# Spreading an ELU chain over two iterations of a fused attention and two-layer expert kernel

## The chip, the cores and the metric

The kernel runs on one core of one Trainium2 chip. The metric is the device time of one launch in microseconds, lower is better; a kernel's time is the median of its runs.

## What is computed

Three stages follow each other, all in float32. The first is attention in chunks of 32 queries, with 8 memory keys and a window of 16 keys to the left and 8 to the right, for 4 batches, 8 heads, 768 tokens and a head size of 64. Its output, 3072 tokens by 512, goes through a feed-forward layer with an ELU, and that through a second layer without one:

```python
h = x @ w_in                                   # 512 -> 2048
g = np.where(h > 0.0, h, np.exp(np.minimum(h, 0.0)) - 1.0)
x = g @ w_out                                  # 2048 -> 512
a = x @ w1
b = x @ w2
out = ((a * b) @ w3) @ w_out2                  # 512 -> 1024 -> 1024 -> 512
```

## The kernel before

**Numbers.** Every float32 operand of a large matmul is split in a high part and a low part, and each product is three matmuls (`mm3`, L129 to L131). The weights arrive as 64-bit numbers: a job of the `feed` (`rebase` L164, `shift` L168, `low` L172, `hi_of` L177, `lo_of` L180) turns the two words of each into float32 and then into the high and low part. ScalarE (ACT) does `rebase` and `hi_of`, VectorE (DVE) the other three. Jobs for the weights of the first layer run while the loop below runs its first iterations. Jobs for the weights of the second layer (`mid_jobs`) are spread between the attention groups, and their results are stored back to DRAM.

**The main loop.** It has 130 iterations n. Each handles one block of 128 of the 2048 inner columns for 384 tokens. `mm_h(n)` makes a block h in one of two PSUM banks (12 matmuls of 384 columns; bank n % 2), `elu_exp(n)` takes it through relu (L484) and exp (L485) on ACT, `elu_split(n)` forms the ELU with a maximum on DVE (L491, called max below; it is the last reader of the bank), its high part on ACT (hi, L125) and its low part on DVE (lo, L126), and `mm_x(n)`, which is issued two iterations later, multiplies the result by w_out. So `mm_h(n + 2)` waits for max(n), and `mm_x(n)` for lo(n).

**What runs between.** Each iteration takes two slots of the attention, one behind `mm_h` and one behind `mm_x` (`at_step`). A group G of 128 queries takes about ten slots: transposes of q and k (`at_turn`, `at_turn2`, copied out by ACT in L298 to L311), scores (L322 on TensorE), maximum, subtraction and exponential (`at_max`: L339 and L340 on DVE, L341 on ACT), sums and normalization (L347 to L359), a transpose on DVE (`at_flip`, L370), the product with v (L381), and the copy into the next block of x (`at_out`). The slots of each group are set by `paces` and `base`; every engine runs its own instructions in the order in which this Python code issues them, and SyncE (SP) issues nearly all DMAs, also in that order.

**Blocks.** After 8 or 16 iterations the 384 tokens of the block are done. In the first two iterations of the next block, called F and F + 1 here, `mm_x` and its slot come ahead of `mm_h` (`first`). In iteration F + 1 the four output banks are copied out (`store_x1`: L120 twice on ACT, L122 twice on DVE) into tiles of the pool `f_p`, which has four buffers and is shared with the weight jobs, and each copy is stored by a DMA (L506). From the sixth block on, the blocks have 16 iterations, and five of them, from iterations 32, 48, 64, 80 and 96, begin with an attention group.

Of the kernel before, what the change touches and what calls it, by code (L numbers as in the profile page):

```python
# [8 lines left out]
F32 = mybir.dt.float32  # L9
F32R = mybir.dt.float32r  # L10
I32 = mybir.dt.int32
AF = mybir.ActivationFunctionType
ALU = mybir.AluOpType
# [6 lines left out]
def tile_kernel(  # L20
# [23 lines left out]
    nc = tc.nc  # L44
    P = 128
# [13 lines left out]
    TB = 384  # L59
    NB = NT // TB  # L60
    GPB = TB // GQ
    FF1 = w_in.shape[1] // P
# [19 lines left out]
    g_p = ctx.enter_context(tc.tile_pool(name="g_p", bufs=3))  # L82
# [41 lines left out]
    def split(hi, lo, src):  # L124
        nc.scalar.copy(hi, src)  # L125
        nc.vector.tensor_tensor(out=lo, in0=src, in1=hi.bitcast(F32), op=ALU.subtract)  # L126
# [314 lines left out]
    others = [Job((raw_rows, w_out2, c, 0), store=wod[c]) for c in range(FF2)]  # L441
# [3 lines left out]
    for G in range(GPB, NG):  # L445
        s0, pace = base(G)
        for at, fn in zip(paces[pace], chain):
            put(s0 + at, fn, G)
        if G >= GM:
            n = [(G - GM + i) * n_others // (NG - GM) for i in range(2)]  # L450
            for job, at in zip([others.pop(0) for _ in range(n[1] - n[0])], (0, 5)):
                mid_jobs.append(job)
                for i, fn in enumerate((rebase, mid_low, mid_split)):
                    put(s0 + at + i, fn, job)
                if at == 0 and w3s and pace == "slow":
                    job = w3s.pop(0)
                    mid_jobs.append(job)
                    for at3, fn in ((3, rebase), (4, mid_low), (9, mid_flip)):
                        put(s0 + at3, fn, job)
    assert not others and not w3s  # L460
    slot_at = [0]
# [1 line left out]
    def at_step():  # L463
        store_next()
        for _, _, fn, arg in sorted(slots.pop(slot_at[0], ()), key=lambda x: x[:2]):
            fn(arg)
        slot_at[0] += 1


    h_t, eg_t, g_t = {}, {}, {}  # L470
# [3 lines left out]
    def mm_h(n):  # L474
        j, f = seq[n][:2]
        ph, w, x = PS[4 + n % 2][:, 0:TB], W[f], xhl[j % 2]
        for i in range(KT):
            c = slice(i * P, (i + 1) * P)
            mm3(ph, w[:, 0, c], w[:, 1, c], x[:, 0, i, :], x[:, 1, i, :], i == 0, i == KT - 1)
        h_t[n] = ph  # L480

    def elu_exp(n):
        e = eg_p.tile([P, TB], F32, tag="eg", name="eg")
        nc.scalar.activation(e, h_t[n], AF.Relu, scale=-1.0)  # L484
        nc.scalar.activation(e, e, AF.Exp, scale=-1.0)  # L485
        eg_t[n] = e

    def elu_split(n):
        ph, e = h_t.pop(n), eg_t.pop(n)
        g = g_p.tile([P, 2, TB], F32R, tag="g", name="g")  # L490
        nc.vector.scalar_tensor_tensor(out=e, in0=e, scalar=-1.0, in1=ph, op0=ALU.add, op1=ALU.max)  # L491
        split(g[:, 0, :], g[:, 1, :], e)
        g_t[n] = g

    def mm_x(n):
        f, at, last = seq[n][1:]
# [83 lines left out]
    with tc.manual_schedule():  # L580
        def weight(i):
            if i < FF1:
                return Job((raw_cols, w_in, i), slot=i)
            return Job((raw_rows, w_out, i - FF1, 0), slot=i)

        jobs, due = [], {}
        order = sorted(range(2 * FF1), key=lambda i: (i % FF1 // HALF, i if i < FF1 else i - FF1 + 2))
        for i in order:
            due[i] = len(jobs)
            jobs.append(weight(i))  # L590
        first_late = min(due[i] for i in LATER)
        feed = Feed(jobs)

        load_qk(0)
        make_identity(nc, ident)
        nc.gpsimd.memset(kn[0:LEFT, 0], 0.0)
        nc.gpsimd.memset(vw[0:LEFT, 0], 0.0)
        for c in range(NCG):
            for s in range(2):
                nc.gpsimd.memset(odd[c * CH:(c + 1) * CH, s], float(c % 2 == s))  # L600
        feed.load(1)
        load_qk(1)
        feed.load(2)
        load_v(0)
        load_qk(2)
        load_v(1)
        feed.load(3)
        load_v(2)
        feed.load(5)
        one = dict(t=at_turn, u=at_turn2, s=at_scores, m=at_max, z=at_sum, n=at_norm, p=at_flip, v=at_values, o=at_out)  # L610
        for what in START.split():
            if what == "f":
                feed.step()
            else:
                one[what[0]](int(what[1]))
        load_qk(GPB)
        load_v(GPB)
        early_psum.close()
        psum_x = ctx.enter_context(tc.tile_pool(name="psum_x", bufs=1, space=PSUM))
        for i in range(KT):  # L620
            PS[i] = psum_x.tile([P, 512], F32, name=f"bank{i}")
        NH = NB * FF1
        for n in range(NH + 2):
            j, f, at, last = seq[n] if n < NH else (NB, n - NH, n - NH, False)
            first = at < 2 and n >= 2
            if j == NB - 1 and f == 0:
                store_next()
                mid_ctx.close()
                at_ctx.close()
                late = ctx.enter_context(tc.tile_pool(name="late", bufs=1, side="right"))  # L630
                ab_jobs = [(c, r) for c in range(FF2) for r in range(2)]
            if n == FF1 + 2:
                feed.until(len(feed.jobs) - 1)
                raw_ctx.close()
                mid_ctx = ExitStack()
                pools["raw"] = mid_ctx.enter_context(tc.tile_pool(name="raw2", bufs=2, side="right"))
                pools["st"] = mid_ctx.enter_context(tc.tile_pool(name="st_p", bufs=2, side="right"))
                mid_load(2)

            def x():  # L640
                if n >= 2:
                    if n < 3 * FF1 // 2 + 2:
                        feed.until(due[FF1 + seq[n - 2][1]])
                    mm_x(n - 2)
                    if at == 1 and n < NH:
                        p = n // HALF - 1
                        store_x1(seq[n - 2][0], x1p if p < 2 else x1d)
                if n < FF1 + 2:
                    feed.step()
                at_step()  # L650

            if first:
                x()
            if n < NH:
                if j == 0:
                    feed.until(due[f])
                mm_h(n)
                elu_exp(n)
                if n < FF1 + 2:
                    feed.step()  # L660
                at_step()
            if not first:
                x()
            if n < NH:
                elu_split(n)
            if n >= NH - FF1:

                free = [f] if n < NH else []
                if n >= NH - FF1 + 2:
                    free.append(FF1 + n - 2 - (NH - FF1))  # L670
                for slot in free:
                    if len(s_wo) < FF2 and len(s_wo) <= len(s_w3):
                        fill(slot, wod[len(s_wo)])
                        s_wo.append(slot)
                    elif len(s_w3) < 2 * FF2:
                        half, c = divmod(len(s_w3), FF2)
                        fill(slot, w3d[half][c])
                        s_w3[half, c] = slot
                    else:
                        c, r = ab_jobs.pop(0)  # L680
                        fill(slot, wabd[c][r])
                        s_ab[c, r] = slot
            if j == NB - 1:
                if f == 4:
                    load_x1(0)
                if f == 8:
                    split_x1(0)
                    load_x1(1)
        store_x1(NB - 1, x1d)
        for half in range(2):  # L690
            for c in range(FF2):
                for i in range(KT):
                    mm_wc(half, c, i)
                    if c == FF2 - 1:
                        keep_wc(half, i)
            for i in range(KT, FF2):
                c, r = ab_jobs.pop(0)
                fill(s_w3[half, i], wabd[c][r])
                s_ab[c, r] = s_w3[half, i]
        NA = NB * FF2  # L700
        for n in range(NA + 1):
            j, f = divmod(n, FF2)
            if n < NA:
                mm_ab(n)
                if f == 2 and j + 1 < NB:
                    split_x1(j + 1)
                    if j + 2 < NB:
                        load_x1(j + 2)
            if n >= 1:
                mm_o(n - 1)  # L710
                if f == 0:
                    store_out(j - 1)
# [30 lines left out]
```

## Time and profile before

| | us |
|---|---|
| median of 3 runs (1163.06 to 1166.07) | 1163.41 |
| profiled execution, its own time | 1165.6 |
| profiled execution, span from first to last instruction | 1163.8 |
| TensorE matmul busy | 1101.9 (95%) |
| TensorE weight load busy | 1038.8 (89%) |
| VectorE busy | 500.8 (43%) |
| ScalarE busy | 432.0 (37%) |

In the rows below, PE is TensorE, PEld its weight load, DVE VectorE, ACT ScalarE and SPq the queue of SyncE. A row of a timeline has the start, the duration, the engine, the line, what it writes and reads, shapes and count, and in brackets how long the engine was idle before it and what ended that. The first 40 us hold the attention of the first three groups; the main loop runs from 39.8 to 713 us, its weight jobs until about 154 us and its attention until about 645 us; the second layer follows. Times of shares are averages over stages with different limits, so the stretches are read apart.

### The profile page before, as it was taken

Reading aid. Unit: us, or ns where it says so; the run is one execution under the profiler, and the core shown is the slowest. Engines: PE = TensorE matmul, PEld = TensorE weight load, DVE = VectorE, ACT = ScalarE, POOL = GpSimd, SP = SyncE. Lnnn points to the kernel's source line nnn. Section 1 sums busy time; section 2 is a strip of 40 time slices with the busy share of each in tenths; the row PEclk is TensorE's granted clock in tenths of the full one; section 3 lists DMA queues with packets and bytes.
Section 4 is the critical chain, followed back from the end, with each engine's and each line's share of the span. In section 5 each row is a group of like instructions: output and inputs, shape, how many; then the busy total and the mean of one; then the engine's idle time right before and its main releaser. Section 6 shows DMA issues by size and latency. Waiting matters only on the chain.

```text
span 1163.8 us, 20920 instructions
## 1 busy us (share of the span) xinstructions
PE 1101.9 (95%) x8800; PEld 1038.8 (89%) x8800; DVE 500.8 (43%) x924; ACT 432.0 (37%) x901; POOL 2.1 (0%) x16
## 2 busy tenths in 40 slices
PE   4667899999999999999999999999999999999998
PEld 3557898989999989989999999799999999999997
DVE  4677745655655655565655341032212212122221
ACT  3444654444545544554454441031212212122111
POOL 0000000000000000000000000000000000000000
PEclk7677999999999999999999999999999999999999
DMA  8934624354454544543542696320100101000000
GB/s 188 253 90 128 205 81 130 118 154 124 141 155 124 153 151 119 158 134 115 167 126 71 232 327 218 109 64 11 44 28 28 55 1 55 28 28 28 1 28 28
DMA packets 155405, 127.94 MB, mean 110 GB/s; under 512 B 104112, under 2 KB 138928, under 8 KB 155312
## 3 DMA queue, kind: packets, MB, share of 16 engines
q1 hardware_dynamic: 154272, 126.35, 36.1%
q8 instruction: 69, 1.13, 0.4%
q10 hardware_dynamic: 1040, 0.26, 0.1%
q14 instruction: 24, 0.20, 0.1%
HBM read 91.46 MB, written 35.13 MB: 109 GB/s over the span
## 4 chain that ended last, share of the span: by engine, by line
PE 84%; DVE 7%; ACT 3%; DMA 2%; issue 2%; SPq 1%; DVEq 0%; ACTq 0%
PE bank L129 22%; PE bank L131 21%; PE bank L130 21%; PE banks L129 4%; PE banks L130 4%; PE banks L131 4%; PE banks L381 2%; PE banks L322 1%; DMA x1d<-st 1%; DVE e L359 1%; DVE w L180 1%; DVE f L172 1%; PE banks L294 1%; PE banks L296 1%; DVE eg L491 1%
## 5 line engine op out<-in xcount | busy, mean ns | idle before, releaser
L129 PE MATMUL bank<-xhl,w 128*128 128x384 f32 x768 | 266.9, 348 | 10.6 <-DVE eg L491 10.0
L131 PE MATMUL bank<-xhl,w 128*128 128x384 f32 x768 | 260.9, 340 | 0.0
L130 PE MATMUL bank<-xhl,w 128*128 128x384 f32 x768 | 260.6, 339 | 0.0
L125 ACT CAST g<-eg 128x384 fp32r<-128x384 f32 x192 | 98.4, 512 | 310.8 <-DVE eg L491 171.7
L129 PE MATMUL bank<-g,w 128*128 128x384 f32 x512 | 178.1, 348 | 0.0
L131 PE MATMUL bank<-g,w 128*128 128x384 f32 x512 | 173.0, 338 | 0.0
L130 PE MATMUL bank<-g,w 128*128 128x384 f32 x512 | 172.9, 338 | 0.0
L126 DVE TENSOR_TENSOR g<-eg,g 128x384 fp32r<-128x384 f32 x192 | 107.2, 558 | 141.9 <-ACT g L125 141.9
L129 PEld LDWEIGHTS bank<-xhl,w 128*128 128x128 f32 x768 | 146.3, 191 | 19.4 <-DVE eg L491 13.6
L561 DVE TENSOR_TENSOR eg<-eg,banks 128x384 f32<-128x384 f32 x64 | 35.5, 555 | 267.2 <-PE banks L131 267.2
L130 PEld LDWEIGHTS bank<-xhl,w 128*128 128x128 f32 x768 | 146.6, 191 | 3.2 <-DVE xhl L126 0.4
L131 PEld LDWEIGHTS bank<-xhl,w 128*128 128x128 f32 x768 | 146.5, 191 | 0.0
L129 PEld LDWEIGHTS bank<-g,w 128*128 128x128 f32 x512 | 97.4, 190 | 2.3
L130 PEld LDWEIGHTS bank<-g,w 128*128 128x128 f32 x512 | 97.6, 191 | 0.0
L131 PEld LDWEIGHTS bank<-g,w 128*128 128x128 f32 x512 | 97.4, 190 | 0.0
L560 ACT COPY eg<-bank 128x384 f32<-128x384 f32 x64 | 30.7, 480 | 168.1 <-PE bank L131 168.1
L484 ACT ACTIVATE eg<-bank 128x384 f32<-128x384 f32 x128 | 62.6, 489 | 67.0 <-PE bank L131 67.0
L491 DVE SCALAR_TENSOR_TENSOR eg<-eg,bank 128x384 f32<-128x384 f32 x128 | 69.7, 545 | 39.0 <-ACT eg L485 38.7
L129 PE MATMUL banks<-xhl,w 128*128 128x384 f32 x256 | 85.5, 334 | 0.0
L130 PE MATMUL banks<-xhl,w 128*128 128x384 f32 x256 | 85.5, 334 | 0.0
L131 PE MATMUL banks<-xhl,w 128*128 128x384 f32 x256 | 85.5, 334 | 0.0
L131 PE MATMUL bank<-w,g 128*128 128x512 f32 x192 | 76.0, 396 | 0.0
(100 smaller groups left out, 1303.6 us busy)
## 6 DMA issues: line engine op xcount, KB each, us to landing
raw<-in_moe_w_dram SPq DMA_DIRECT2D x32, 512.0 KB
raw<-in_moe_w_out_dram SPq DMA_DIRECT2D x19, 512.0 KB
w3d<-st SPq DMA_DIRECT2D x16, 512.0 KB
wabd<-st SPq DMA_DIRECT2D x16, 512.0 KB
w<-w3d SPq DMA_DIRECT2D x16, 512.0 KB
w<-wabd SPq DMA_DIRECT2D x16, 512.0 KB
raw<-in_moe_w_in_dram SPq DMA_DIRECT2D x13, 512.0 KB
x1d<-st SPq DMA_DIRECT2D x32, 192.0 KB
```

What stands on the lines that cost most here:

```text
L125: nc.scalar.copy(hi, src)
L126: nc.vector.tensor_tensor(out=lo, in0=src, in1=hi.bitcast(F32), op=ALU.subtract)
L129: mm(o, lhsT=w_hi, rhs=x_hi, start=start, stop=False)
L130: mm(o, lhsT=w_hi, rhs=x_lo, start=False, stop=False)
L131: mm(o, lhsT=w_lo, rhs=x_hi, start=False, stop=stop)
L172: nc.vector.scalar_tensor_tensor(out=t, in0=l, scalar=29, in1=t, op0=ALU.logical_shift_right, op1=ALU.bitwise_or)
L180: nc.vector.tensor_tensor(out=job.to[:, 1, :], in0=job.f if src is None else src, in1=job.to[:, 0, :].bitcast(F32), op=ALU.subtract)
L381: mm(o, lhsT=vw[cc, u, 2 * hp + r, :], rhs=pT[cc, r, hp, u, :], start=u == 0, stop=u == 1)
L484: nc.scalar.activation(e, h_t[n], AF.Relu, scale=-1.0)
L491: nc.vector.scalar_tensor_tensor(out=e, in0=e, scalar=-1.0, in1=ph, op0=ALU.add, op1=ALU.max)
L560: nc.scalar.copy(e, pab[0])
L561: nc.vector.tensor_tensor(out=e, in0=e, in1=pab[1], op=ALU.mult)
```

## The change

The chain of one block h is no longer issued at the end of one iteration. Relu and exp of block n move behind the attention slot that follows `mm_h(n)`; max stays at the end of the iteration; hi and lo of block n move into iteration n + 1, right behind `mm_h(n + 1)`, with a step of the weight feed between them while there is one. The second mid job of a group starts one slot later (6 for 5), and `rebase` and `low` of its job for w3 one slot later (4 and 5 for 3 and 4). The instructions themselves, their shapes and TensorE's order are the same.

```diff
-            for job, at in zip([others.pop(0) for _ in range(n[1] - n[0])], (0, 5)):
+            for job, at in zip([others.pop(0) for _ in range(n[1] - n[0])], (0, 6)):
...
-                    for at3, fn in ((3, rebase), (4, mid_low), (9, mid_flip)):
+                    for at3, fn in ((4, rebase), (5, mid_low), (9, mid_flip)):
...
-    def elu_split(n):
-        ph, e = h_t.pop(n), eg_t.pop(n)
-        g = g_p.tile([P, 2, TB], F32R, tag="g", name="g")
-        nc.vector.scalar_tensor_tensor(out=e, in0=e, scalar=-1.0, in1=ph, op0=ALU.add, op1=ALU.max)
-        split(g[:, 0, :], g[:, 1, :], e)
-        g_t[n] = g
+    def elu_max(n):
+        e = eg_t[n]
+        nc.vector.scalar_tensor_tensor(out=e, in0=e, scalar=-1.0, in1=h_t.pop(n), op0=ALU.add, op1=ALU.max)
+
+    def elu_hi(n):
+        g_t[n] = g_p.tile([P, 2, TB], F32R, tag="g", name="g")
+        nc.scalar.copy(g_t[n][:, 0, :], eg_t[n])
+
+    def elu_lo(n):
+        g = g_t[n]
+        nc.vector.tensor_tensor(out=g[:, 1, :], in0=eg_t.pop(n), in1=g[:, 0, :].bitcast(F32), op=ALU.subtract)
...
                 mm_h(n)
+            if 1 <= n <= NH:
+                elu_hi(n - 1)
+            if n < FF1 + 2:
+                feed.step()
+            if 1 <= n <= NH:
+                elu_lo(n - 1)
+            at_step()
+            if n < NH:
                 elu_exp(n)
-                if n < FF1 + 2:
-                    feed.step()
-                at_step()
             if not first:
                 x()
             if n < NH:
-                elu_split(n)
+                elu_max(n)
```

In the changed kernel max is L490, hi is L494 and lo is L498. Three places show what moves.

ACT in iteration 1, from the attention's exponential (L341) on; `eg` is the tile of the ELU, `w` a weight's tile, `f` the working tile of a weight job. Before:

```order
L341 ACTIVATE e<-e 128x512
L125 CAST g<-eg 128x384
L484 ACTIVATE eg<-bank_96 128x384
L485 ACTIVATE eg<-eg 128x384
L177 CAST w_85<-f 128x512
L164 ACTIVATE f<-more 128x512
```

and now:

```order
L341 ACTIVATE e<-e 128x512
L494 CAST g<-eg 128x384
L177 CAST w_85<-f 128x512
L164 ACTIVATE f<-more 128x512
L484 ACTIVATE eg<-bank_96 128x384
L485 ACTIVATE eg<-eg 128x384
```

The weight job's two instructions stood behind relu and exp of block 1 and now stand ahead of them.

ACT in iteration 48, the first of a block (F), from the copies of the turned q on. Before, hi of block 47 stood first:

```order
L125 CAST g<-eg 128x384
L298 COPY qT<-banks 128x512
L301 COPY kT<-banks 128x16x32
L302 COPY kT<-banks 128x4x3x24
L164 ACTIVATE f<-raw 128x512
L484 ACTIVATE eg<-bank_95 128x384
```

and now:

```order
L298 COPY qT<-banks 128x512
L301 COPY kT<-banks 128x16x32
L302 COPY kT<-banks 128x4x3x24
L164 ACTIVATE f<-raw 128x512
L494 CAST g<-eg 128x384
L309 COPY kT<-banks 128x4x24
L311 COPY kT<-banks 128x16x8
L484 ACTIVATE eg<-bank_95 128x384
```

Hi of block 47 moved behind three copies of the attention and a `rebase`.

ACT in iteration 49 (F + 1), from the copies of the outputs (`st`) on. Before:

```order
L120 COPY st<-bank_597 128x384
L120 COPY st<-bank_599 128x384
L177 CAST st<-f 128x512
L484 ACTIVATE eg<-bank_96 128x384
L485 ACTIVATE eg<-eg 128x384
L341 ACTIVATE e<-e 128x512
L164 ACTIVATE f<-raw 128x512
L125 CAST g<-eg 128x384
```

and now:

```order
L120 COPY st<-bank_597 128x384
L120 COPY st<-bank_599 128x384
L177 CAST st<-f 128x512
L494 CAST g<-eg 128x384
L341 ACTIVATE e<-e 128x512
L484 ACTIVATE eg<-bank_96 128x384
L485 ACTIVATE eg<-eg 128x384
L494 CAST g<-eg 128x384
L164 ACTIVATE f<-raw 128x512
```

Relu and exp of block 49 moved behind the attention's exponential L341, and hi of block 48 came down from the iteration before.

## Rows read from the trace of the kernel before

**Rows 1.** Busy time by stretch: us, each engine's busy (x), clock, DMA share, GB/s.

```profile
110.47:154.00 43.53, 39.45 (x256) 38.35 (x257) 33.15 (x62) 28.14 (x55) 0.00 (x0) 0.90 0.53 159
245.00:650.00 405.00, 399.12 (x4076) 381.43 (x4076) 230.60 (x430) 197.77 (x421) 0.00 (x0) 1.00 0.45 134
```

**Rows 2.** Waits of PE from 250 to 650: us in total, times, longest.

```profile
PE bank L129 <- DVE eg L491: 5.9, 6, 1.3
```

**Rows 3.** Timeline of ACT in the first two iterations.

```profile
44.46 0.49 ACT L484 ACTIVATE eg<-bank 128x384 f32<-128x384 f32 x1 [4.71 <-PE bank L131]
...
52.30 0.49 ACT L125 CAST g<-eg 128x384 fp32r<-128x384 f32 x1
54.37 0.49 ACT L484 ACTIVATE eg<-bank 128x384 f32<-128x384 f32 x1 [1.57 <-PE bank L131]
...
55.33 0.60 ACT L177 CAST w<-f 128x512 fp32r<-128x512 f32 x1
```

**Rows 4.** Timeline of DVE at the same place.

```profile
55.97 0.69 DVE L180 TENSOR_TENSOR w<-f,w 128x512 fp32r<-128x512 f32 x1 [1.51 <-ACT w L177]
```

**Rows 5.** Timeline of PE, at the products with v of three groups.

```profile
62.10 0.38 PE L381 MATMUL banks<-pT,vw 64*64 64x64 f32 x4 [5.50 <-DVE pT L370]
...
110.47 0.39 PE L381 MATMUL banks<-pT,vw 64*64 64x64 f32 x4 [4.08 <-DVE pT L370]
...
213.38 0.34 PE L381 MATMUL banks<-pT,vw 64*64 64x64 f32 x7 [0.96 <-DVE pT L370]
```

**Rows 6.** Timeline of ACT in iteration 5.

```profile
92.99 0.49 ACT L484 ACTIVATE eg<-bank 128x384 f32<-128x384 f32 x1 [1.24 <-PE bank L131]
...
95.02 0.56 ACT L298 COPY qT<-banks 128x512 f32<-128x512 f32 x1
```

**Rows 7.** Timeline of DVE in iterations 10 and 11.

```profile
136.39 0.55 DVE L491 SCALAR_TENSOR_TENSOR eg<-eg,bank 128x384 f32<-128x384 f32 x1
137.52 0.56 DVE L126 TENSOR_TENSOR g<-eg,g 128x384 fp32r<-128x384 f32 x1 [0.58 <-ACT g L125]
...
141.33 0.55 DVE L491 SCALAR_TENSOR_TENSOR eg<-eg,bank 128x384 f32<-128x384 f32 x1
```

**Rows 8.** Timeline of DVE at the block that begins with iteration 48.

```profile
330.43 0.56 DVE L122 COPY st<-bank 128x384 f32<-128x384 f32 x1 [2.97 <-ACT eg L484]
...
332.45 0.69 DVE L340 TENSOR_TENSOR e<-banks,mx 128x512 f32<-128x512 f32 x1
333.06 0.55 DVE L491 SCALAR_TENSOR_TENSOR eg<-eg,bank 128x384 f32<-128x384 f32 x1
334.80 0.56 DVE L126 TENSOR_TENSOR g<-eg,g 128x384 fp32r<-128x384 f32 x1 [1.20 <-ACT g L125]
...
338.79 0.55 DVE L491 SCALAR_TENSOR_TENSOR eg<-eg,bank 128x384 f32<-128x384 f32 x1
```

**Rows 9.** Timeline of PE at the same block, iteration 52.

```profile
339.39 0.44 PE L129 MATMUL bank<-xhl,w 128*128 128x384 f32 x1 [1.17 <-DVE eg L491]
```

**Rows 10.** Timeline of ACT at the same block.

```profile
319.96 0.51 ACT L125 CAST g<-eg 128x384 fp32r<-128x384 f32 x1 [1.22 <-DVE eg L491]
...
323.36 0.68 ACT L164 ACTIVATE f<-raw 128x512 f32<-128x512 f32 x1
...
329.94 0.49 ACT L484 ACTIVATE eg<-bank 128x384 f32<-128x384 f32 x1 [2.26 <-PE bank L131]
330.46 0.53 ACT L485 ACTIVATE eg<-eg 128x384 f32<-128x384 f32 x1
333.18 0.63 ACT L341 ACTIVATE e<-e 128x512 f32<-128x512 f32 x1 [2.19 <-DVE e L340]
```

**Rows 11.** Issues of SP at the same block.

```profile
325.60 0.37 SPq L145 DMA_DIRECT2D raw<-in_moe_w_dram  x1
326.81 4.53 SPq L506 DMA_DIRECT2D x1d<-st  x4
```

**Rows 12.** Waits of DVE from 245 to 600: us in total, times, longest.

```profile
DVE st L122 <- DMA x1d<-st: 13.5, 4, 4.1
```

**Rows 13.** Timeline of DVE at the block that begins with iteration 96.

```profile
573.55 0.56 DVE L122 COPY st<-bank 128x384 f32<-128x384 f32 x1 [2.00 <-DMA x1d<-st]
```

**Rows 14.** Busy time of PE by stretch, as rows 1.

```profile
132.06:135.20 3.14, 3.14 (x13) 0.67 0.47 160
118.30:128.80 10.50, 10.50 (x62) 1.00 0.68 227
```

## The prediction

> **What bounds the kernel now.** I looked first at busy time by stretch, since the change touches only the main loop. From 245 to 650 us TensorE is busy for 399.1 of 405 us at the full clock, while VectorE and ScalarE are busy for about half [rows 1]. So there the change can win at most the few stalls of TensorE, and the list of its waits holds one cause, 5.9 us in six waits for max to free a bank of h [rows 2]. The rest is to be had before 154 us, where the timelines show TensorE waiting for VectorE and these two for ScalarE. I read the timelines at the two kinds of place where TensorE stalls: the ramp (40 to 154 us), where weight jobs compete with the ELU, and the starts of blocks.
>
> **The ramp: what is removed.** ScalarE's queue runs in order, and relu(n) is the one instruction in it that waits for `mm_h(n)`: 4.71 us in iteration 0, 1.57 in iteration 1 [rows 3]. What stands behind waits too: in iteration 1 the cast L177 of a weight starts at 55.33, and VectorE waits for it until 55.97 [rows 3, 4], with the attention's sums, normalization and transpose behind; TensorE gets the transposed tile only at 62.10 after 5.50 us of idling [rows 5].
>
> Term 1. In the new order L177 follows hi(0) directly. Hi starts at 52.30; the maximum behind which it waits comes some 0.4 us earlier, because relu(0) no longer holds the first copies. So hi starts at 51.9, L177 at 52.3 instead of 55.33, 3.0 us earlier. VectorE now does lo(0) behind that cast, 0.5 us, which leaves 2.5 us at L381: 59.6 for 62.10.
>
> Term 2. From there to the next group's product each lo loses its wait for hi, because a weight step stands between them now; two such waits of about 0.6 us, less some delay of a weight cast behind relu and exp, leave 0.8 us. Sum 3.3.
>
> Term 3. In iteration 5 the copy L298 runs at 95.02 behind relu (92.99, waiting for TensorE), exp and a weight step [rows 6]. It needs only transposes that TensorE runs right behind the block whose end released relu, so by about 93.4, and now it stands ahead of relu: 1.6 us. Another shorter wait of lo gives 0.5. At 110.47 [rows 5] the gain is 5.4 us.
>
> Term 4. From iteration 10 to 15 VectorE sets the pace: from max to max 4.94 us, with only one idle piece of 0.58, lo waiting for hi [rows 7]. With a weight step between them that piece goes, and 4.36 us remain; TensorE's own two blocks of 12 matmuls take 4.1 (62 in 10.5 us at the full clock [rows 14]), so VectorE still sets it. Four iterations give 2.3 us. The ramp gains 5.4 + 2.3 = 7.7 us. As bounds I take 5 (terms 1 and 4 alone) and 9.5 (blocks like that at 132.06, which ran at 0.67 of the clock [rows 14], might be spared it).
>
> **Behind the ramp** no step of the feed stands between hi and lo, so VectorE waits for hi as before, and nothing is won in the middle of a block: TensorE has no wait there. What is moved is relu and exp, behind the attention slot, and max with them.
>
> **The starts of blocks: what is added.** In iteration F + 1 VectorE's second copy of the outputs must wait until the DMA of the first copy has landed; four of the five starts show it as such, 13.5 us in all [rows 12], the fifth under another name: 2.97 us until 330.43 [rows 8]. With it the scores' maximum and L340 wait (332.45) and ScalarE's L341 (333.18) [rows 8, 10]. Before, relu and exp of block F + 1 (329.94, 330.46) ran while VectorE waited [rows 10], so max(F + 1) went right behind L340, at 333.06. Now they stand behind L341. From the copy at 330.43, t0, step by step: L340 at 2.0, plus lo(F), which now also stands behind the copy, 0.5: t0 + 2.5. L341 0.73 later (332.45 to 333.18): 3.2. L341, relu and exp at 0.5 each, and 0.1: max(F + 1) at t0 + 4.85. Lo(F + 1) starts 1.13 behind max, as in [rows 7]: 5.98. From lo to max(F + 2) the work is unchanged, 334.80 to 338.79, 3.99: t0 + 9.97. Before it was 338.79 - 330.43 = 8.36. So max(F + 2) is 1.6 us later, and the matmul that already waits for it, `mm_h(F + 4)` at 339.39 [rows 9], with it; queued behind that are the group's L381 and all that follows.
>
> And t0 itself moves. Hi(F - 1) ran at 319.96 and now stands behind the rebase at 323.36, so at 323.9 [rows 10]; lo(F - 1) behind it starts at about 324.5 and pushes the weight job's work, and with it the load issued at 325.60, by 0.9 us, while the first store, issued at 326.81 [rows 11], moves by 0.1 only. If the landing goes by the store's own issue, t0 moves 0.1; if the load ahead of it in the queue sets it, 0.9. I take 0.6, nearer to the load, since load and store leave 1.2 us apart on one queue and land together only 3.6 us later.
>
> [...]
>
> Per start 1.6 + 0.6 = 2.2 us, five starts 11.0 us. The start at iteration 96 has no TensorE wait in the trace, but max there is done just before its matmul, so it pays nearly all. As bounds for one start: 1.0 (the two L120 no longer stand behind hi(F), so the store could leave and land 0.6 earlier) and 2.7.
>
> One group more, at 213.38 [rows 5]: its L340 stands in the same iteration as an output copy, lo(24) now waits for a hi behind L341 and holds the sums. That adds 0.9 us (bounds 0 and 1).
>
> **Edits at nothing.** The jobs that start one slot later issue the same instructions and loads; before 650 us VectorE is idle for 43% of the time [rows 1], which hides them. Without that cover one slip of L168 and L172 would cost about 1 us in a group. The number of instructions, TensorE's order and the second layer stay.
>
> **Sum.** -7.7 + 11.0 + 0.9 = +4.2 us, on the profiled execution's own 1165.6: 1169.8 us. That execution is 2.2 above the median of 1163.41, so I forecast **1167.6 us**.
>
> **Rivals.**
> 1. The two sides cancel. If a start costs only its lower bound, 1.1 with the change of t0, five give 5.5: -7.7 + 5.5 + 0.9 = -1.3, 1162.1 us. For it: the store's copies do come free of hi(F). Against it: the load's delay, and that relu behind L341 is in the order itself.
> 2. Faster: the starts cost next to nothing, because the store lands early. At iteration 96 the same copy waited 2.00 us [rows 13], against up to 4.1 at the others [rows 12]; if the earlier copies let all stores land so, t0 would fall by about 1.5 us and pay for the longer chain: -7.7 + 0.9 = -6.8, 1156.6 us. It decides from a cost per start under 0.7 us. Against it: load and store stand closer together on the queue, not further apart.
> 3. Slower still: TensorE's clock. After a wait of 3.15 us at 132 us the next 3.14 us ran at 0.67 of the clock and the block took 3.14 instead of 2.03 [rows 14], 1.1 us lost. After the present waits of up to 1.3 us at block starts the clock stays at 1.00 [rows 1, 2]. With several waits of 0.6 to 1.5 us in a row at each start it might fall: 5 x 1.1 = 5.5 us more, 1173.1.
>
> [...] The trace at block starts does not agree so far, hence its low chance.
>
> **How the numbers follow.** Less than 0.3%, 3.5 us, can hardly be told from no change here. Forecast 0.50, its own range 1164 to 1172; rival 1 0.24; rival 2 0.15; rival 3 0.11. Faster takes rival 2 and a little of 1: 0.19. Same takes the rest of 1 and the low edge of the forecast: 0.27. Slower is 0.54. The range of 1157 to 1173.5 leaves out about half of rival 3 and a part of rival 2.
>
> **What the profile would show.** Right: L381 near 59.6 and 105 us; lo without a wait in the ramp; iteration 15's block some 7 to 8 us earlier; then at each of the five starts relu directly behind L341, max(F + 1) about 2 us later against the output copy, and TensorE's waits for max (now L490) grown from 6 to about 15 us or more, some under `mm_x` waiting for lo (L498). Wrong: waits of TensorE at the starts unchanged or gone; a ramp that ends no earlier, with a new wait for relu in it; a clock under 1.00 behind 245 us; or stalls in the middle of blocks, where max now follows the attention's work.

## The result: slower by 0.65%, a ramp that gains and block starts that lose more

| | us |
|---|---|
| before, median of 5 runs beside the changed kernel | 1163.41 (1159.81 to 1166.07) |
| after, median of 5 runs | 1170.6 (1169.24 to 1172.9) |
| ratio, with its 95% interval | 1.0065 [1.0042, 1.0089] |
| after, profiled execution: own time, span | 1170.6, 1168.8 |

First the busy time by stretch of the kernel after, with the columns of [rows 1], and its waits of TensorE from 250 to 650 us, as [rows 2]:

```profile
110.47:154.00 43.53, 40.73 (x219) 40.16 (x218) 31.74 (x59) 26.80 (x53) 0.00 (x0) 0.93 0.47 145
245.00:650.00 405.00, 391.97 (x3960) 371.69 (x3959) 229.16 (x425) 196.32 (x413) 0.00 (x0) 1.00 0.44 131
```

```profile
PE bank L129 <- DVE eg L490: 10.9, 10, 1.4
PE bank L130 <- DVE g L498: 0.9, 2, 0.5
```

From 245 us on TensorE is busy 7 us less than in [rows 1], at the same clock of 1.00. Its waits for max have nearly doubled against [rows 2], from 5.9 to 10.9 us and from six to ten, two at each of the five starts, and waits for lo are new.

**The ramp.** TensorE at the products with v, against [rows 5]:

```profile
61.52 0.37 PE L381 MATMUL banks<-pT,vw 64*64 64x64 f32 x4 [4.44 <-DVE pT L370]
...
106.57 0.38 PE L381 MATMUL banks<-pT,vw 64*64 64x64 f32 x4 [3.51 <-DVE pT L370]
...
124.62 0.44 PE L129 MATMUL bank<-g,w 128*128 128x384 f32 x1 [1.38 <-ACT g L494]
126.47 0.69 PE L130 MATMUL bank<-g,w 128*128 128x384 f32 x1 [1.42 <-DVE g L498]
...
207.81 0.29 PE L381 MATMUL banks<-pT,vw 64*64 64x64 f32 x4 [0.64 <-DVE pT L370]
```

The three products with v come 0.6, 3.9 and 5.6 us earlier than before. In between stand two waits that [rows 5] has no partner for: at 124.62 for hi, at 126.47 for lo. ScalarE in iterations 1 and 5, against [rows 3, 6]:

```profile
53.85 0.50 ACT L494 CAST g<-eg 128x384 fp32r<-128x384 f32 x1
54.26 0.61 ACT L177 CAST w<-f 128x512 fp32r<-128x512 f32 x1
54.78 0.67 ACT L164 ACTIVATE f<-more 128x512 f32<-128x512 f32 x1
55.35 0.47 ACT L484 ACTIVATE eg<-bank 128x384 f32<-128x384 f32 x1
...
90.14 0.58 ACT L298 COPY qT<-banks 128x512 f32<-128x512 f32 x1 [1.40 <-PE banks L296]
...
92.33 0.51 ACT L484 ACTIVATE eg<-bank 128x384 f32<-128x384 f32 x1
```

L177 follows hi, and L298 stands ahead of relu. Relu waits for nothing in either place; in [rows 3, 6] it held the queue for 1.57 and 1.24 us. VectorE at the cast of [rows 4], and at max in iterations 9, 10 and 13 (against [rows 7]):

```profile
54.90 0.69 DVE L180 TENSOR_TENSOR w<-f,w 128x512 fp32r<-128x512 f32 x1 [0.16 <-ACT w L177]
...
126.62 0.55 DVE L490 SCALAR_TENSOR_TENSOR eg<-eg,bank 128x384 f32<-128x384 f32 x1 [0.20 <-ACT eg L485]
...
131.02 0.55 DVE L490 SCALAR_TENSOR_TENSOR eg<-eg,bank 128x384 f32<-128x384 f32 x1
...
144.20 0.55 DVE L490 SCALAR_TENSOR_TENSOR eg<-eg,bank 128x384 f32<-128x384 f32 x1
```

The wait of 1.51 us at L180 has shrunk to 0.16, and from max to max it is now 4.40 us (131.02 - 126.62; four intervals take 17.58).

**A start of a block**, iteration 48, as [rows 8 to 12]. VectorE first, then TensorE, ScalarE, the issues, and VectorE's waits from 245 to 600 us:

```profile
327.43 0.56 DVE L122 COPY st<-bank 128x384 f32<-128x384 f32 x1 [4.16 <-DMA x1d<-st]
...
328.75 0.53 DVE L498 TENSOR_TENSOR g<-eg,g 128x384 fp32r<-128x384 f32 x1
...
329.92 0.69 DVE L340 TENSOR_TENSOR e<-banks,mx 128x512 f32<-128x512 f32 x1
332.30 0.55 DVE L490 SCALAR_TENSOR_TENSOR eg<-eg,bank 128x384 f32<-128x384 f32 x1 [1.69 <-ACT eg L485]
333.44 0.56 DVE L498 TENSOR_TENSOR g<-eg,g 128x384 fp32r<-128x384 f32 x1 [0.58 <-ACT g L494]
...
337.55 0.55 DVE L490 SCALAR_TENSOR_TENSOR eg<-eg,bank 128x384 f32<-128x384 f32 x1
```

```profile
332.91 0.45 PE L129 MATMUL bank<-xhl,w 128*128 128x384 f32 x1 [1.38 <-DVE eg L490]
...
338.15 0.44 PE L129 MATMUL bank<-xhl,w 128*128 128x384 f32 x1 [0.81 <-DVE eg L490]
```

```profile
330.70 0.63 ACT L341 ACTIVATE e<-e 128x512 f32<-128x512 f32 x1 [6.24 <-DVE e L340]
331.24 0.47 ACT L484 ACTIVATE eg<-bank 128x384 f32<-128x384 f32 x1
331.75 0.52 ACT L485 ACTIVATE eg<-eg 128x384 f32<-128x384 f32 x1
```

```profile
322.71 0.37 SPq L145 DMA_DIRECT2D raw<-in_moe_w_dram  x1
323.19 2.06 SPq L511 DMA_DIRECT2D x1d<-st  x2
```

```profile
DVE st L122 <- DMA x1d<-st: 15.7, 4, 4.2
```

Relu and exp, which ran in the shadow of the store's landing in [rows 10], now stand behind L341 while ScalarE idles 6.24 us ahead of it. From the copy at 327.43 max(F + 2) takes 10.12 us, for 8.36 in [rows 8]. That is 1.76 more, and it is 1.76 more at each of the other four starts too, when the same two rows are read there. The store leaves 0.48 us behind the load, for 1.21 in [rows 11].

### The profile page after: what moved, and what is told of

It reads as the page before. It is cut to its first block, busy times and chain, and to the rows that moved or that the text cites. A ratio compares the mean times of both kernels' runs of the same rounds, so it can differ in the third digit from the quotient of the medians.

```text
span 1168.8 us, 20946 instructions
## 1 busy us (share of the span) xinstructions
PE 1104.1 (94%) x8800; PEld 1038.0 (89%) x8800; DVE 500.8 (43%) x924; ACT 434.5 (37%) x901; POOL 2.1 (0%) x16
## 4 chain that ended last, share of the span: by engine, by line
PE 83%; DVE 7%; DMA 4%; ACT 4%; issue 2%; SPq 1%; DVEq 0%; ACTq 0%
PE bank L129 22%; PE bank L130 21%; PE bank L131 21%; PE banks L129 4%; PE banks L130 4%; PE banks L131 4%; PE banks L381 2%; DMA x1d<-st 2%; PE banks L322 1%; DMA kn<-in_k_dram 1%; DVE g L498 1%; DVE e L359 1%; PE banks L296 1%; PE banks L294 1%; PE banks L308 1%
## 5 line engine op out<-in xcount | busy, mean ns | idle before, releaser
L129 PE MATMUL bank<-xhl,w 128*128 128x384 f32 x768 | 265.7, 346 | 11.6 <-DVE eg L490 10.9
L498 DVE TENSOR_TENSOR g<-eg,g 128x384 fp32r<-128x384 f32 x128 | 71.3, 557 | 101.1 <-ACT g L494 101.1
L494 ACT CAST g<-eg 128x384 fp32r<-128x384 f32 x128 | 65.7, 513 | 124.9 <-DVE eg L490 124.9
L490 DVE SCALAR_TENSOR_TENSOR eg<-eg,bank 128x384 f32<-128x384 f32 x128 | 69.8, 545 | 57.7 <-ACT eg L485 57.4
```

The source lines that it names most:

```text
L129: mm(o, lhsT=w_hi, rhs=x_hi, start=start, stop=False)
L494: nc.scalar.copy(g_t[n][:, 0, :], eg_t[n])
L498: nc.vector.tensor_tensor(out=g[:, 1, :], in0=eg_t.pop(n), in1=g[:, 0, :].bitcast(F32), op=ALU.subtract)
```

## The experiments

All twelve were timed in several runs beside the kernel before, on one chip for each set of four (before: 1162.24, 1162.14 and 1161.52 us). All fourteen kernels run the same 8800 matmuls in the same order, so one time can be read at the same matmul in each trace. **A** is the L381 at 213.38 of [rows 5], and its time is what the ramp costs. **B** is a matmul near the end of the main loop (690.72 us before, 695.76 after). Between A and B lie the five starts. From B to its last matmul every execution takes the same 468.9 us.

| kernel | median us | ratio to before | A | A to B |
|---|---|---|---|---|
| before | 1163.4 | 1 | 213.4 | 477.4 |
| after | 1170.6 | 1.0065 [1.0042, 1.0089] | 207.8 | 488.0 |
| e1 new order in the ramp only | 1155.6 | 0.9948 [0.9930, 0.9966] | 205.9 | 474.1 |
| e2 new order behind the ramp only | 1175.5 | 1.0118 [1.0101, 1.0135] | 213.1 | 487.6 |
| e3 exp ahead of the attention step | 1157.7 | 0.9968 [0.9955, 0.9981] | 202.5 | 479.2 |
| e4 hi and lo ahead of the copies | 1168.8 | 1.0058 [1.0037, 1.0079] | 207.0 | 487.1 |
| e5 exp ahead of the feed's step too | 1170.7 | 1.0074 [1.0061, 1.0086] | 218.0 | 478.8 |
| e6 before, packed copies | 1156.1 | 0.9951 [0.9937, 0.9964] | 211.4 | 468.1 |
| e7 after, packed copies | 1152.5 | 0.9917 [0.9904, 0.9931] | 208.5 | 471.0 |
| e8 e1, packed copies | 1148.5 | 0.9885 [0.9871, 0.9899] | 204.8 | 468.1 |
| e9 before, exp behind the feed's step | 1156.2 | 0.9947 [0.9927, 0.9966] | 204.9 | 474.1 |
| e10 before, new job slots | 1162.1 | 1.0001 [0.9988, 1.0014] | 210.7 | 474.3 |
| e11 e9, packed copies | 1150.9 | 0.9905 [0.9884, 0.9926] | 207.6 | 468.1 |
| e12 e3, packed copies | 1149.6 | 0.9893 [0.9874, 0.9912] | 205.6 | 470.5 |

One execution's A is uncertain. Four programs with the order of before up to there have 213.4, 211.4, 210.7 and 213.1 (mean 212.2); five with the new order have 204.8 to 208.5 (mean 206.8). A part of that is TensorE's clock: from the first to the second product of [rows 5] the order of before took 48.4 and 49.1 us in two executions where the granted clock in between was 0.82 and 0.81, and 45.5 and 45.7 us in two where it was 0.88 and 0.87. The execution of before that was costed is one of the first two; why its clock was lower was not looked into. A to B repeats within 0.5 us for an order, with one exception: the profiled execution of before, 477.4, where three others of the same order there have 474.1 to 474.3.

**e1 and e2: the two halves apart.** The new order stands while `n < FF1 + 2` (18, as long as the feed runs) in e1, whose lines against the changed kernel follow, and only from there on in e2, with the two branches exchanged; the job slots are those of the order behind the ramp:

```diff
+            if n < FF1 + 2:
+                if n >= 1:
+                    elu_hi(n - 1)
                 feed.step()
+                if n >= 1:
+                    elu_lo(n - 1)
+                at_step()
...
+            else:
...
+                if n < NH:
+                    elu_exp(n)
+                at_step()
...
                 elu_max(n)
+                if n >= FF1 + 2:
+                    elu_hi(n)
+                    elu_lo(n)
```

> The new order of the ELU's steps (and of the job slots) only as long as the feed runs, iterations 0 to 17; from iteration 18 on the order and the slots of before. Theory: the change is two separate effects, a gain in the ramp and a loss at the five starts of blocks. Then this kernel keeps the gain that the changed kernel showed by 213 us, 5.6 us, and pays nothing behind it: 1163.4 - 5.6 = 1157.8 us, ratio 0.995. Rival A: the earlier end of the ramp is of no use, since loads of the middle part then come too late and TensorE waits for them: about 1163. Rival B: the loss at the starts comes from the ramp (what was moved forward collides there), not from the order behind it: about 1170.

> The order of before in iterations 0 to 17, the new order (and the new job slots) from 18 on. Theory: pays the five starts in full and gains nothing: 1163.4 + 10.4 = 1173.8 us, ratio 1.009; TensorE's stall for the maximum at each start grows from about 1 to about 3 us in two pieces. Rival: if the starts are dear only because the ramp ended earlier, about 1163.

Measured: 1155.6 and 1175.5. TensorE's waits from 245 to 650 us in e2:

```profile
PE bank L129 <- DVE eg L490: 10.8, 10, 1.4
PE bank L130 <- DVE g L498: 2.2, 6, 0.9
```

Both rivals of e1 and that of e2 fall: the gain and the loss are separate, and they add: -0.52% and +1.18% give +0.66%, where the whole change has +0.65%. e2's loss is above what I expected, 13.3 us between the medians for 10.4.

**e3 and e4: which of the moves the starts pay for.** e3 puts one line of the changed kernel back; e4 puts hi and lo back ahead of the output copies in iterations F and F + 1:

```diff
+            if n < NH:
+                elu_exp(n)
             at_step()
-            if n < NH:
-                elu_exp(n)
```

```diff
+            early = first and n >= FF1 + 2
+            if early and n <= NH:
+                elu_hi(n - 1)
+                elu_lo(n - 1)
             if first:
                 x()
...
-            if 1 <= n <= NH:
+            if 1 <= n <= NH and not early:
                 elu_hi(n - 1)
...
-            if 1 <= n <= NH:
+            if 1 <= n <= NH and not early:
                 elu_lo(n - 1)
```

> The changed kernel with one line moved back: relu and the exponential ahead of the attention step again; the maximum stays at the iteration's end, the two parts of g stay in the next iteration. My sum has 1.6 us per start for relu and exp behind L341 together with the low part behind the output copy; the low part alone is 0.5 of these. Theory: the place of the exponential is the larger half of the start's cost, so of 10.4 us some 5 to 6 are won back in five starts, less what relu in ScalarE's queue costs again in the ramp (1.6 us for iteration 5, perhaps all of the 5.6): 1165 to 1168 us. Rival: the starts are dear because the output copy's wait (t0) moved, so the place of the exponential does not count: at the starts nothing changes, 1170 us or above.

> The changed kernel, but in the first two iterations of a block from iteration 18 on (where x and the output copies stand ahead) the two parts of g of the iteration before are made ahead of the output copies, as they were in the kernel before; the exponential stays behind the attention step. Theory: the low part no longer stands behind the copy that waits for the landing (0.5 per start), and the load no longer slips ahead of the first store (0.6 per start): 5 x 1.1 = 5.5 us won, 1165 us. Rival: all of the cost lies in relu and exp behind L341: 1170 us, no change. [...]

e3 gave 1157.7, 11 us less than the changed kernel by the two ratios (13 by the medians) and below the 1165 to 1168 that I expected; its rival falls. VectorE and ScalarE at iteration 48 in e3:

```profile
320.13 0.56 DVE L122 COPY st<-bank 128x384 f32<-128x384 f32 x1 [4.05 <-DMA x1d<-st]
...
321.45 0.53 DVE L498 TENSOR_TENSOR g<-eg,g 128x384 fp32r<-128x384 f32 x1
...
323.23 0.55 DVE L490 SCALAR_TENSOR_TENSOR eg<-eg,bank 128x384 f32<-128x384 f32 x1
...
328.53 0.55 DVE L490 SCALAR_TENSOR_TENSOR eg<-eg,bank 128x384 f32<-128x384 f32 x1
```

```profile
319.45 0.49 ACT L484 ACTIVATE eg<-bank 128x384 f32<-128x384 f32 x1 [2.19 <-PE bank L131]
```

Relu runs ahead of the landing again, and from the copy to max(F + 2) it takes 8.40 us, as before the change, although lo(F) still stands behind the copy. Max(F + 1) pays the 0.5 for it, but lo(F + 1) then waits 0.64 for its hi in place of 1.20 in [rows 8], so nothing arrives at max(F + 2). e4 keeps the exponential behind L341 and moves little: 1168.8, with an interval that overlaps the changed kernel's; A to B is 0.9 us shorter where 5.5 were expected. Its chain shrinks to 9.64 us, and from the first store's issue to the copy it takes 3.78 us on average where the changed kernel takes 4.34. But the copies now stand behind hi and lo, and TensorE's waits are no shorter in sum. Behind the two longest of them, which end at 248.92 and 498.96 us, TensorE also ran at a granted clock of 0.50 and 0.51 for 3.4 us, which happened at none of the five starts of the changed kernel (the last two rows have the columns of [rows 1]):

```profile
PE bank L129 <- DVE eg L490: 12.9, 8, 3.3
```

```profile
248.92 0.44 PE L129 MATMUL bank<-xhl,w 128*128 128x384 f32 x1 [3.08 <-DVE eg L490]
```

```profile
249.80:253.20 3.40, 3.40 (x13) 3.40 (x12) 3.23 (x9) 1.08 (x3) 0.00 (x0) 0.50 0.00 0
498.90:502.30 3.40, 3.34 (x10) 3.35 (x11) 2.69 (x7) 2.00 (x4) 0.00 (x0) 0.51 0.00 0
```

In the changed kernel's trace matmuls of 384 columns start every 0.32 us where the clock is 0.51 (from 127.28 us) and every 0.17 us where it is 1.00 (from 130.03 us), so by my estimate the two stretches cost some 3 us together. The place of the exponential costs 12.9 us between A and B (487.1 - 474.2), some 3 of them by the clock, the place of hi and lo 5.0 (479.2 - 474.2), and both together 13.8. Without the clock's part the two come close to adding up; that they share one wait is not shown.

**e5 and e9: which of the moves the ramp gains by.** e5 puts the exponential back ahead of the feed's step, with hi and lo still in the next iteration (against the changed kernel). e9 is the opposite, the kernel before with this line alone moved (against the kernel before):

```diff
+            if n < NH:
+                elu_exp(n)
             if n < FF1 + 2:
                 feed.step()
             if 1 <= n <= NH:
                 elu_lo(n - 1)
             at_step()
-            if n < NH:
-                elu_exp(n)
```

```diff
                 mm_h(n)
-                elu_exp(n)
                 if n < FF1 + 2:
                     feed.step()
+                elu_exp(n)
                 at_step()
```

> The changed kernel with relu and the exponential back at their place in the kernel before, ahead of the feed's step and so ahead of the weight casts in ScalarE's queue; the parts of g stay in the next iteration, the maximum stays at the end. The run with the exponential ahead of the attention step but behind the feed's step gave 1157.7 us. Theory (terms 1 and 3 of the prediction, L177 in iteration 1 and L298 in iteration 5 out from behind relu, 2.5 and 1.6 us): these 4.1 us are lost, 1161.8 us, the starts of blocks are as in that run. Rival: the whole gain of the ramp comes from lo no longer waiting for hi (terms 2 and 4) and relu's place in ScalarE's queue is of no weight: 1157.7 us.

> The kernel before with one line moved: relu and the exponential behind the feed's step instead of ahead of it, still ahead of the attention step; maximum and both parts of g stay together at the end, the slots as before. Behind iteration 17 nothing differs from before. So far: both moves with the exponential behind the feed's step gave 1157.7 us, the parts of g moved alone gave 1170.7. Theory: relu, which waits for TensorE, ahead of the weight casts in ScalarE's queue is what the ramp loses by; its place alone brings most of the ramp's gain of 6.6 us: 1156 to 1158 us. Rival: the gain needs both moves, since the low part still waits for the high part (2.3 us by term 4 and 0.8 + 0.5 in terms 2 and 3): about 1159.5 us.

e5 gave 1170.7, 13 us above e3 and 9 above what the theory asked for; e9 gave 1156.2, as much as e1 by the ratios, from one line. ScalarE in iteration 1 of e9, and TensorE at the first and third product:

```profile
51.63 0.62 ACT L177 CAST w<-f 128x512 fp32r<-128x512 f32 x1
52.15 0.68 ACT L164 ACTIVATE f<-more 128x512 f32<-128x512 f32 x1
53.29 0.49 ACT L484 ACTIVATE eg<-bank 128x384 f32<-128x384 f32 x1 [0.47 <-PE bank L131]
```

```profile
59.43 0.29 PE L381 MATMUL banks<-pT,vw 64*64 64x64 f32 x4 [3.75 <-DVE pT L370]
...
102.62 0.38 PE L381 MATMUL banks<-pT,vw 64*64 64x64 f32 x4 [4.07 <-DVE pT L370]
```

That is the step of the prediction's term 1 by itself. Of term 3 only a part is in it: L298 still stands behind relu and exp (at 87.20 us), but relu, behind a weight step now, waits for nothing there. Nor is it all that the ramp can give. In e9 TensorE still waits 0.50 us for max in four iterations from 128 to 144 us, the idle piece of term 4; in e3, whose hi and lo stand in the next iteration besides, these waits are gone. The mean A of e3 and e12 is 204.1 us, that of e9 and e11 206.3, of the new order 206.8. So in the ramp hi and lo in the next iteration gain about 2 us beside a relu and exp that stand between the feed's step and the attention step, and moving these two behind the attention step gives 2.7 us back. In e5 the other half by itself makes a wait of its own. ScalarE, VectorE and TensorE of e5 around 122 us:

```profile
121.23 0.49 ACT L484 ACTIVATE eg<-bank 128x384 f32<-128x384 f32 x1 [3.20 <-PE bank L131]
121.76 0.52 ACT L485 ACTIVATE eg<-eg 128x384 f32<-128x384 f32 x1
122.19 0.60 ACT L177 CAST w<-f 128x512 fp32r<-128x512 f32 x1
```

```profile
122.82 0.69 DVE L180 TENSOR_TENSOR w<-f,w 128x512 fp32r<-128x512 f32 x1 [2.64 <-ACT w L177]
123.43 0.55 DVE L498 TENSOR_TENSOR g<-eg,g 128x384 fp32r<-128x384 f32 x1
```

```profile
124.03 0.69 PE L130 MATMUL bank<-g,w 128*128 128x384 f32 x1 [2.66 <-DVE g L498]
```

Read it backwards: TensorE waits for lo, which stands behind L180, which waits for L177, which stands behind exp and relu, and relu waited for TensorE's last block. The same wait comes back five times up to 159 us, with 0.39 to 0.65 us. So moving lo behind a weight step helped only where the exponential stood behind that step as well (e3 for e5).

**e6, e7, e8: the landing of the store.** From iteration 32 on, the fourth bank is copied in three pieces of 128 columns into unused columns of the first three output tiles, so no copy waits for a tile to come free:

```diff
+    def store_packed(j, to):
+        ts = []
+        for o in range(KT - 1):
+            t = f_p.tile([P, 512], F32, tag="f", name="st")
+            ts.append(t)
+            copy_on("av"[o % 2], t[:, 0:TB], PS[o][:, 0:TB])
+            nc.sync.dma_start(out=to[j][:, o, :], in_=t[:, 0:TB])
+        for o, t in enumerate(ts):
+            c = slice(o * P, (o + 1) * P)
+            nc.vector.tensor_copy(t[:, TB:512], PS[KT - 1][:, c])
+            nc.sync.dma_start(out=to[j][:, KT - 1, c], in_=t[:, TB:512])
...
-                        store_x1(seq[n - 2][0], x1p if p < 2 else x1d)
+                        put_x1 = store_packed if n >= 2 * FF1 else store_x1
+                        put_x1(seq[n - 2][0], x1p if p < 2 else x1d)
```

> The kernel before, but from iteration 32 on the fourth bank's 384 columns are copied in three pieces of 128 into spare columns of the first three output tiles, so no copy waits for a store to land (two VectorE copies and two stores more per block). Theory: the landing of the store sets t0 and with it the stalls at four of the five starts. They sum to 5.9 us here at all starts, 3.9 us in an execution with shorter landings: 1162.2 - 3 to 4 = 1158 to 1159 us. Rival: with the wait gone the chain of L339, L340 and the ELU is as long as before and TensorE waits for the same: 1162 us, or more for the added copies.

> The changed kernel with the same packed output copies from iteration 32 on. Theory: relu and the exponential behind L341 are dear only because VectorE has stood still until the store landed; without that wait four of five starts lose their added 2 us and some of the old stall: 1170.6 - 4 x 2.1 - 3 = 1159 us, within 3 us of the run with the exponential moved back (1157.7). Rival: the place of the exponential costs by itself, landing or not: the two packed kernels then lie as far apart as the unpacked ones (7 to 8 us), and this one is at 1166 us or above.

> The new order in iterations 0 to 17 only, the order and slots of before behind it, and the packed output copies from iteration 32 on. Theory: both gains add, the ramp's (1155.6 us measured without packing) and the packing's 3 to 4 us: 1152 us. Rival: packing gives nothing, 1155.6 us.

1156.1, 1152.5 and 1148.5: all below what the theory asked for. TensorE's waits from 245 to 650 us in e7, and its busy time there in e8:

```profile
PE bank L130 <- DVE g L498: 0.6, 4, 0.2
```

```profile
245.00:650.00 405.00, 405.00 (x4070) 390.00 (x4069) 230.66 (x437) 201.43 (x426) 0.00 (x0) 1.00 0.47 142
```

Without the wait for the landing TensorE does not stop once from 245 to 650 us in e8. From A to B packing gives the order of before 6.1 us and the new order 17.0 (488.0 - 471.0), so the two orders are 2.9 us apart where they were 13.8. The rival of e7 falls: the late exponential is dear because VectorE has stood still until the store landed, and what then follows is on the path that TensorE waits for.

**e10, e11, e12: what was left.** e10 is the kernel before with the two rows of slots alone; e11 is e9 and e12 is e3, both with the packed copies of the diff above:

```diff
-            for job, at in zip([others.pop(0) for _ in range(n[1] - n[0])], (0, 5)):
+            for job, at in zip([others.pop(0) for _ in range(n[1] - n[0])], (0, 6)):
...
-                    for at3, fn in ((3, rebase), (4, mid_low), (9, mid_flip)):
+                    for at3, fn in ((4, rebase), (5, mid_low), (9, mid_flip)):
```

> The kernel before with only the two rows of job slots changed, (0, 6) for (0, 5) and (4, 5, 9) for (3, 4, 9). Theory: these edits are free, 1162 us, within 0.15%. Rival: a weight job that starts one slot later collides with the groups' sums, about 1 us in some of the twenty groups behind the ramp: 1165 us or more.

> The run with only the exponential's place changed, and with the packed output copies from iteration 32 on. Theory: both gains add, as they did with the new order of the ramp (1148.5 us): 1162.1 - 6.1 (packing alone) - 4 to 6 = 1150 to 1152 us. If the place of the exponential alone brings all of the ramp's gain, 1148 to 1149.

> The changed kernel with the exponential ahead of the attention step (behind the feed's step) and with the packed output copies. Theory: at the starts nothing is left to lose, so it ends as the kernel with the new order in the ramp alone and packed copies (1148.5 us), where the changed kernel with packed copies, exponential behind the attention step, ended 4 us later (1152.5): 1148 to 1149.5 us. Rival: the 4 us belong to the parts of g in the next iteration, which this kernel still has: 1152 us.

e10: 1162.1, no change, its rival falls. e11: 1150.9, within what was expected. e12: 1149.6; its A to B, 470.5, is e7's and not e8's. So the 2.4 to 2.9 us that remain without the landing belong to hi and lo in the next iteration, which the rival said; its median lies lower than the rival's all the same, for a ramp that ends earlier. e8, e11 and e12 have overlapping intervals; 0.9885 for e8 is the best seen. e3's order in the ramp, the old order behind it and packed copies together were not run.

## Why the prediction was right, step by step

The verdict and the two sides were right: 1170.6 for 1167.6, inside the forecast's own range, with a ramp that gains less than the starts lose. Most sizes were off by 1 to 3 us. Against the means of several executions the ramp was put 2.3 too high and the starts 2.8 too low, and the 0.9 for the group at 213.38 did not come: 4.2 us for the 3.0 that were missing. The rest is within the spread of the medians of before (1161.5 to 1163.4).

- **Term 1** (2.5 us at 62.10) was 0.6 in the profiled execution. There q and k landed late: TensorE waits 0.80 us for the group's q and 0.38 for its k (0 and 0.17 before) and starts on q at 45.48, for 44.22 before. From that matmul to the product the new order takes 1.75 us less (15.9, mean of five executions, for 17.7 of four), the exponential's place alone (e9, e11) 2.0 less. The mechanism is shown; the size was 0.5 to 0.8 too large, and what takes the rest was not looked into.
- **Terms 1 to 3** together (5.4 at 110.47): 3.9 in the profiled pair, 4.6 between the means of four and five executions. Term 2's and term 3's part for lo (0.8 and 0.5) is not seen in this order: e9 and e11 leave lo where it was and gain as much, and e5, which moves only hi and lo, gains nothing there (111.14). It is seen with relu and exp ahead of the attention step, where e3 and e12 come 1.0 us earlier on average than e9 and e11. What the terms left out is what relu and exp behind the attention step cost in the ramp: 1.9 us up to there by the same means (104.9 for 103.0).
- **Term 4** (2.3): right in its place and mostly given back next to it. Max to max fell from 4.94 to 4.40 for a predicted 4.36, 2.2 us in four intervals. But the ramp has block starts of its own. In iteration 9 hi(8) now stands behind the second output copy, which waits 2.60 us for a store, and lo(8) behind a weight step, and TensorE waits 1.38 and 1.42 us for them (124.62 and 126.47), 2.8 in all; from 126.4 to 129.8 us the granted clock is then 0.51. The order of before has one wait at this start, for max:

```profile
132.06 0.45 PE L129 MATMUL bank<-xhl,w 128*128 128x384 f32 x1 [3.15 <-DVE eg L491]
```

It is gone (that matmul runs at 130.03 without a wait), so the new waits stand in its place and not on top of it. My sum had neither. From 110.47 to 151.80 the new order gains only 0.3 us on average, 1.2 in the profiled pair.
- **The ramp in all:** 7.7 predicted; 5.6 in the profiled pair, 5.4 between the means at A, within my bounds of 5 and 9.5.
- **The chain of a start** (1.6, max(F + 2) at t0 + 9.97): 1.76, at t0 + 10.12, at five starts of five. One part of the working was wrong: lo(F) behind the copy costs nothing at max(F + 2) by itself (e3); relu and exp behind L341 cost it all.
- **t0** (0.6 per start): from the first store's issue to the copy it took 3.94 us on average in the profiled execution of before and 4.34 after, so 0.4; whether the load or the store sets it stays open (last section). The starts together: 10.6 us from A to B for a predicted 11.0.
- That agreement is partly luck. Against the three other executions with the old order from A on, the starts cost 13.8: there the same landing took 3.43 us on average, and 1.76 + 0.9 a start gives 13.3. The execution that I costed had late landings. This is the larger of the two errors; I had set its 2.2 us above the median down to the whole and not to the starts.
- **The group at 213.38** (+0.9): did not come, its wait fell from 0.96 to 0.64. Why was not tested; to the sum it matters 1 us.
- **Edits at nothing:** held (e10).
- **Rivals.** Cancelling (a start at 1.1 us or less) and early stores fall with e2. Of rival 3, the clock fell at no start behind the ramp: 1.00 from 245 to 650 us, with waits of up to 1.4 us. It did fall in the ramp, behind the two waits of 1.38 and 1.42 us with one matmul between them (0.51 from 126.4 to 129.8 us), and behind waits of 3.08 and 3.31 us in e4 (0.50 and 0.51). What decides whether a lower clock follows a wait is not shown: at the starts it did not after up to 1.4 us, in the ramp it did after 1.38 and 1.42.

What the change was worth can therefore be had by one line of it: the exponential behind the weight step, as long as there are weight steps (e9, 0.9947). Hi and lo in the next iteration gave some 2 us more in the ramp beside that line (e3, e12) and lost 6 without it (e5: A 218.0 for a mean of 212.2). Behind the attention step the exponential pays 9 us at the block starts (488.0 for e3's 479.2), and that in turn hangs on a copy that waits for a store (e7).

## What to carry to other kernels

In an engine's queue, an instruction that waits for the busiest engine did better here behind work that waits for nothing (relu behind the weight step: e9, 0.9947), but not behind work that was itself late (relu behind L341 at the block starts: 488.0 us from A to B for e3's 479.2); both answers occurred in one kernel, so an order that suits the ramp need not suit the steady part. Where a step loses its place in the shadow of a wait, look at the wait first: taking it away gave 6.1 us between A and B (e6), where no order that kept it went below the 474.1 us of the old one. And before a stall is priced from one execution, its size should be read in two or three: here the same five starts cost 3 us more in the one that was profiled.

## What was not expected of the hardware

The time from a first store's issue on SP until VectorE's waiting copy could go on went with how close a load was ahead of it in the same queue. Where the load left 0.44 to 0.48 us earlier (21 such copies in five kernels, the new order mostly) it was 3.99 to 4.79 us, never less. Where it left 1.0 to 2.2 us earlier (24 copies in five kernels) it was 2.00 to 4.90. At iteration 48 the copy moved by 3.00 us between before and after, as the load's issue did (2.89), and not as the store's (3.62). That one start would suit a landing that goes with the load. The others do not settle it: at iteration 32 the copy moved by 5.48 us as the store's issue did (5.46), and not as the load's (4.40). And from load to copy it took from 3.8 to 6.3 us in these kernels, so the load is not all that counts, and the rest stays open.
